# Weights of four expert units and the first pass's token operands made by VectorE in feed-forward blocks 2 and 3

## The chip, the cores and the metric

One core of a Trainium2 chip runs the whole program. The metric is the device time in microseconds. TensorE does the matrix products, VectorE, ScalarE and GpSimd the elementwise work, and SyncE (SP) issues every DMA, in one queue, in order. In rows of the profile TensorE is PE (its weight loads PEld), VectorE DVE, ScalarE ACT, GpSimd POOL, and SP's queue SPq.

## The reference, cut to what matters

Three layers follow one another: a chunked attention, a gated feed-forward layer, and a mixture of eight experts that is balanced over all tokens and so needs the logits of all of them.

```python
# attention: 4 batches, 8 heads, 768 positions, 64 wide; chunks of 32 with a window and 8 memory slots
x = softmax(q_c @ k_full.T / 8) @ v_full             # 3072 tokens x 512
# feed-forward, 512 -> 1536 -> 512
x = (sigmoid(x @ w_gate) * (x @ w_val)) @ w_out
# experts, 8 of them, 512 -> 1024 -> 512
P = exp(x @ w_gate2 - max)
for _ in range(8):                                    # balanced over rows and over all 3072 tokens
    P /= P.sum(1) + 1e-9;  P /= P.sum(0) + 1e-9;  P *= 3072 / 8
out = sum(P[:, e] * (relu(x @ w1[e]) @ w2[e]) for e in range(8))
```

## The kernel before, in words

**Precision.** Every float32 operand of a product is split in two: ScalarE writes the rounded high part, and VectorE or GpSimd subtracts it from the source for the low part (`operand`). A product is then three matmuls: high by high, high by low, low by high. Large products go by a scheme with seven products of half-sized blocks instead of eight, so sums and differences of blocks (`combine`) are made ahead of the splits. The seven operands have numbers 0 to 6.

**Stages.** Tokens come in eight chunks of 384. Attention of a chunk is four head pairs. The feed-forward layer works in blocks of two chunks: block 0 plainly, blocks 1, 2 and 3 by the seven products, each in six pairs of hidden columns. A pair b_p is a gate product, a value product (`strassen`), and one pair later the second product (`second`, banks px), whose drains VectorE adds into x2. Attention of the chunks ahead is spread over the blocks by `schedule`, which puts steps of a generator at counts of a clock that `hook` advances, some ten per pair. In block 1 the feed-forward weights are made and stored, in blocks 2 and 3 they are only loaded. A finished chunk of x2 is stored to DRAM (x2d), and its expert logits are made (pl, pm).

The experts come in three passes s of 1024 tokens. In a pass there are 32 units (expert, half, pair of columns); the first layer (`layer1`) makes seven products p of a unit, the second (`layer2` in pass 0, `layer2_turned` after it) takes two units at a time. In pass 0 each unit's raw weights are loaded (`ask`, tiles r), summed on VectorE (wq, wv), split by ScalarE and GpSimd, used, and stored in DRAM (w1k, seven tiles; w2k, four). Passes 1 and 2 load them from there (`w1_load`, w2_get). The token operands of a pass are made by `x_operands`: per pass four parts of 256 columns, each with four sums (xq) and seven splits (xl); the splits of operands 5, 1, 4 and 3 go to GpSimd, the others to VectorE. The balancing (`sinkhorn`) is a chain of small steps of VectorE with a matmul (pm, pb, pc) between them, one step every three products.

**Order.** A scheduler sets the order within each engine from its own timeline; the engines then run in that order and wait on semaphores. Attention's and the feed-forward layer's pools (c1) close at the end of block 3, and the experts' pools (c2) open in their memory, w2p, gg, ps_h and ps_y among them. The raw weights of pass 0 land in gg.

Of the kernel before, what the change touches and what calls it, by code (L numbers as in the profile page):

```python
# [10 lines left out]
F32 = mybir.dt.float32  # L11
# [48 lines left out]
def moe_chain(ctx: ExitStack, tc: tile.TileContext, qkv, mask, mrow, mone, wa, wg, wb, out):  # L60
# [66 lines left out]

    def w1_operands(nm, r, pool, kept=None, ce=None):
        a11, a12, a21, a22 = (r[i][:, kh * 256:(kh + 1) * 256] for i in range(2) for kh in range(2))
        t = w1_tiles(nm, pool)  # L130
        ge = nc.gpsimd
        ce = ce or ge
# [12 lines left out]
        return w1_sets(t)  # L145

    def w1_load(nm, pool, kept):
# [3 lines left out]
        return w1_sets(t)  # L151

    with ExitStack() as c1:
        wc = c1.enter_context(tc.tile_pool(name="wc", bufs=7))
        wp = c1.enter_context(tc.tile_pool(name="wp", bufs=6))
        un = c1.enter_context(tc.tile_pool(name="un", bufs=2))
        at = c1.enter_context(tc.tile_pool(name="at", bufs=2))
        cm = c1.enter_context(tc.tile_pool(name="cm", bufs=1))
        tq = c1.enter_context(tc.tile_pool(name="tq", bufs=5))
# [4 lines left out]

        wgs = cm.tile([128, KD, 2 * E], F32R, name="wgs")
        nc.scalar.copy(wgs[:, :, 0:E], wgate)
# [206 lines left out]
        def gated(nm, v, sg):  # L373
            nc.vector.tensor_tensor(out=v, in0=v, in1=sg, op=ALU.mult)
            gh = gp.tile([128, CT], F32R, tag="gh", name=f"gh{nm}")
            gl = gp.tile([128, CT], F32R, tag="gl", name=f"gl{nm}")
            operand(gh, gl, nc.vector, v)
            return gh, gl

        anchor = []  # L380
# [157 lines left out]
        def second(b, p, x2b, state, halves=(0, 1)):  # L538
            wo, gs = state
            for t in halves:  # L540
# [12 lines left out]
                if p == NPAIR - 1:  # L553
                    store_x2(2 * b + t, x2b[:, :, t, :])

        pend = []
# [58 lines left out]
    with ExitStack() as c2:  # L615
        sk = c2.enter_context(tc.tile_pool(name="sk", bufs=1))
        w2p = c2.enter_context(tc.tile_pool(name="w2p", bufs=8))
        gg = c2.enter_context(tc.tile_pool(name="gg", bufs=1))
        ps_h = c2.enter_context(tc.tile_pool(name="ps_h", bufs=4, space=PS))
        ps_y = c2.enter_context(tc.tile_pool(name="ps_y", bufs=4, space=PS))  # L620

# [51 lines left out]
        SW = 512  # L673
        SHB = 8

        def x_operands(s):
            xop = [[[slot("w" if i in (2, 3, 4) else "x", f"x{h}{s}_{i}_{kk}", 512, F32R) for kk in range(2)]
                    for h in "hl"] for i in range(7)]
            for kk in range(2):
                for o in range(0, 512, XW):  # L680
                    xr = rw.tile([128, 2, 2, XW], F32, tag="r", name=f"xs{s}_{kk}_{o}")
                    for kh in range(2):
                        for tb in range(2):
                            for q in range(0, XW, 128):
                                c, w = divmod(s * SB + tb * 512 + o + q, CT)
                                nc.sync.dma_start(out=xr[:, kh, tb, q:q + 128],
                                                  in_=x2d[c][:, 2 * kh + kk, w:w + 128])
                    b11, b12, b21, b22 = (xr[:, kh, tb, :] for kh in range(2) for tb in range(2))
                    xh = [xop[i][0][kk][:, o:o + XW] for i in range(7)]
                    xl = [xop[i][1][kk][:, o:o + XW] for i in range(7)]  # L690
                    ve = nc.vector
                    q = quad(f"xq{s}_{kk}_{o}")
                    combine(ve, q[:, 0], b12, b11, ALU.subtract)
                    combine(ve, q[:, 1], b22, q[:, 0], ALU.subtract)
                    combine(ve, q[:, 2], b22, b12, ALU.subtract)
                    combine(ve, q[:, 3], b21, q[:, 1], ALU.subtract)
                    for i, src in ((0, b11), (5, q[:, 1]), (1, b21), (6, q[:, 2]), (4, q[:, 0]), (2, b22), (3, q[:, 3])):
                        operand(xh[i], xl[i], nc.gpsimd if i in XP else ve, src)
            return xop
# [12 lines left out]
        def raw_pair(nm, src):  # L712
            rs = []
            for f, k in enumerate(("sh", "sl")):
                rs.append(gg.tile([128, 512], F32, tag=k, name=f"{nm}_{f}", bufs=SHB))
# [27 lines left out]
        def w2_get(s, e, hf, fp):  # L743
            nm = f"{s}_{e}_{hf}_{fp}"
            kept = w2k[e, hf, fp]
            dh, dl = w2_tile(nm, "a"), w2_tile(nm, "b")
            if s == 0:
                rs = raws.pop((e, hf, fp))[1]
# [6 lines left out]
            nc.sync.dma_start(out=dh.bitcast(F32), in_=kept[0])  # L755
            nc.sync.dma_start(out=dl.bitcast(F32), in_=kept[1])
            th, tl = w2_tile(nm, "c"), w2_tile(nm, "d")
            nc.sync.dma_start(out=th.bitcast(F32), in_=kept[2])
# [3 lines left out]
        def g_tile(kind, nm):  # L762
            return gg.tile([128, 512], F32R, tag=kind, name=nm, bufs=DB if kind[0] == "d" else SHB)

# [13 lines left out]
        def layer1(s, e, hf, xop, gs, w2):  # L778
# [6 lines left out]
            for fp in range(2):  # L785
                nm = f"{s}_{e}_{hf}_{fp}"
                if s == 0:
# [59 lines left out]
        def layer2(s, e, hf, gs, w2, acc):  # L847
# [23 lines left out]
            for t in range(NTT):  # L871
# [10 lines left out]
                accumulate(t, acc[t], py, True)  # L882
                if t % 4 == 1:
                    w2_sums()
# [141 lines left out]
```

## Time and profile before

| | |
|---|---|
| median of three runs | 2708.83 us (2707.37 to 2710.35) |
| profiled execution, span from first to last instruction | 2714.6 us |
| busy: PE, PEld, DVE, ACT, POOL | 97%, 83%, 76%, 42%, 30% |
| DMA | 587 MB, 216 GB/s over the span |

The profiled execution lists its span alone; what lies around it is not in the trace. The span is itself 5.8 us above the median of the timed runs. The stages follow from the names in the timeline: feed-forward blocks 2 and 3 lie at about 450 to 785 us, pass 0 of the experts starts at 785 us, pass 1 at about 1460, pass 2 at about 2072. A busy share says little by itself, since matmuls overlap: what TensorE lost in a stretch is told by the number of matmuls in it beside the number in an undisturbed stretch of the same kind.

### The profile page before, as it was taken

The page shows a single profiled execution, that of the slowest core. Times are in us where ns is not written, and L with a number is a line of the kernel's source. Part 1 is how long each engine was busy: PE and PEld are TensorE (multiplying, and loading weights), DVE is VectorE, ACT ScalarE, POOL GpSimd, SP SyncE. Part 2 cuts the span into 40 slices and gives each one's busy share as a digit, 9 for nine tenths or more (in the row PEclk, how much of TensorE's full clock was granted, in tenths as well). Part 3 has the DMA queues.
Part 4 walks back from the last instruction along what each step waited for, and adds up shares of the span by engine and source line. Part 5 has one row for each costly group of instructions (what it writes and reads, how often), then busy time and mean ns, then how long its engine had stood idle before and what let it go on. Part 6 is the DMA issues. An engine that isn't in the chain of part 4 may idle for free.

```text
span 2714.6 us, 37960 instructions
## 1 busy us (share of the span) xinstructions
PE 2646.4 (97%) x12917; PEld 2241.2 (83%) x12917; DVE 2072.3 (76%) x3403; ACT 1130.5 (42%) x2516; POOL 820.3 (30%) x594
## 2 busy tenths in 40 slices
PE   8999999999978999999999999999999999999998
PEld 6898888999967888888888888888887887888887
DVE  7888788675588666666667788888788778888887
ACT  6666866664344334334334333233233332333232
POOL 0002441000045355455453322233234332323232
PEclk9899999999989999999999999999999999999999
DMA  5445677566558476676677556655666565556654
GB/s 203 161 164 207 230 244 256 191 199 206 183 199 288 176 265 244 223 270 242 223 257 248 183 214 228 227 186 201 230 231 226 213 232 201 188 216 233 218 177 171
DMA packets 260526, 586.97 MB, mean 216 GB/s; under 512 B 28873, under 2 KB 45961, under 8 KB 260332
## 3 DMA queue, kind: packets, MB, share of 16 engines
q1 hardware_dynamic: 260332, 584.54, 61.0%
q8 instruction: 102, 1.67, 0.3%
q14 instruction: 92, 0.75, 0.1%
HBM read 408.17 MB, written 176.26 MB: 215 GB/s over the span
## 4 chain that ended last, share of the span: by engine, by line
PE 85%; DVE 8%; DMA 4%; ACT 1%; issue 1%; SPq 0%; POOL 0%; DVEq 0%; ACTq 0%; POOLq 0%
PE p L802 10%; PE p L803 10%; PE p L804 10%; PE py L74 4%; PE pz L901 4%; PE py L75 4%; PE py L76 4%; PE pz L902 4%; PE pz L903 4%; PE pzr L903 3%; PE pzr L901 3%; PE pzr L902 3%; DMA w2b<-w2k 2%; PE px L75 2%; PE px L76 2%; PE px L74 2%
## 5 line engine op out<-in xcount | busy, mean ns | idle before, releaser
L802 PE MATMUL p<-xh,w 128*128 128x512 f32 x1344 | 521.3, 392 | 10.0 <-ACT ce L824 4.9
L803 PE MATMUL p<-xl,w 128*128 128x512 f32 x1344 | 525.9, 391 | 0.8 <-DVE xl L111 0.8
L804 PE MATMUL p<-xh,w 128*128 128x512 f32 x1344 | 520.4, 391 | 0.0
L802 PEld LDWEIGHTS p<-xh,w 128*128 128x128 f32 x1344 | 253.8, 189 | 65.0 <-ACT ce L824 5.8
L803 PEld LDWEIGHTS p<-xl,w 128*128 128x128 f32 x1344 | 253.9, 189 | 54.1 <-DVE xl L111 1.2
L804 PEld LDWEIGHTS p<-xh,w 128*128 128x128 f32 x1344 | 253.8, 189 | 53.4 <-DMA w<-w1k 0.2
L111 POOL TENSOR_TENSOR gl<-ce,gh 128x512 fp32r<-128x512 f32 x64 | 93.2, 1456 | 460.1 <-ACT gh L110 460.1
L909 DVE TENSOR_TENSOR acc<-pz,acc 128x512 f32<-128x512 f32 x248 | 169.7, 686 | 70.9 <-PE pz L903 68.8
L111 POOL TENSOR_TENSOR sl<-cb,sh 128x512 fp32r<-128x512 f32 x64 | 87.1, 1361 | 387.1 <-ACT sh L110 288.3
L74 PE MATMUL py<-w2a,gh 128*128 128x512 f32 x512 | 201.4, 393 | 0.8 <-DVE acc L864 0.8
L75 PE MATMUL py<-w2b,gh 128*128 128x512 f32 x512 | 200.6, 392 | 0.0
L76 PE MATMUL py<-w2a,gl 128*128 128x512 f32 x512 | 197.5, 391 | 0.0
L909 DVE TENSOR_TENSOR acc<-pzr,acc 128x512 f32<-128x512 f32 x248 | 164.7, 686 | 35.8 <-PE pzr L903 34.9
L824 ACT COPY ce<-p 128x512 f32<-128x512 f32 x96 | 56.3, 587 | 224.4 <-PE p L804 215.2
L111 POOL TENSOR_TENSOR w2d<-wv,w2c 128x1024 fp32r<-128x1024 f32 x32 | 77.8, 2430 | 208.5 <-ACT w2c L110 206.6
L864 DVE SCALAR_TENSOR_TENSOR acc<-py,logit,acc 128x512 f32<-128x512 f32 x112 | 80.0, 742 | 71.3 <-PE py L76 71.2
L111 POOL TENSOR_TENSOR xl<-xq,xh 128x256 fp32r<-128x256 f32 x36 | 30.8, 868 | 334.1 <-ACT xh L110 329.0
L818 ACT COPY cb<-p 128x512 f32<-128x512 f32 x96 | 55.8, 581 | 162.4 <-PE p L804 162.4
L807 DVE TENSOR_TENSOR cd<-p,ce 128x512 f32<-128x512 f32 x96 | 66.1, 689 | 68.8 <-ACT ce L824 65.2
L74 PEld LDWEIGHTS py<-w2a,gh 128*128 128x128 f32 x512 | 97.0, 189 | 21.3 <-DVE acc L864 1.2
L76 PEld LDWEIGHTS py<-w2a,gl 128*128 128x128 f32 x512 | 97.0, 189 | 20.3
L75 PEld LDWEIGHTS py<-w2b,gh 128*128 128x128 f32 x512 | 97.0, 189 | 20.0
(289 smaller groups left out, 7025.2 us busy)
## 6 DMA issues: line engine op xcount, KB each, us to landing
w<-w1k SPq DMA_DIRECT2D x448, 256.0 KB
w1k<-w SPq DMA_DIRECT2D x224, 256.0 KB
r<-in_wb SPq DMA_DIRECT2D x128, 256.0 KB
w2a<-w2k SPq DMA_DIRECT2D x64, 512.0 KB
w2b<-w2k SPq DMA_DIRECT2D x64, 512.0 KB
w2c<-w2k SPq DMA_DIRECT2D x64, 512.0 KB
w2d<-w2k SPq DMA_DIRECT2D x64, 512.0 KB
w_g<-wak SPq DMA_DIRECT2D x84, 256.0 KB
```

The source lines that it names most:

```text
L74: nc.tensor.matmul(ps, wh, xh, start=first, stop=False)
L75: nc.tensor.matmul(ps, wh, xl, start=False, stop=False)
L76: nc.tensor.matmul(ps, wl, xh, start=False, stop=last)
L111: return eng.tensor_tensor(out=l, in0=src, in1=h.bitcast(F32), op=ALU.subtract)
L802: nc.tensor.matmul(ps, wh[:, ks], xh, start=kk == 0 and not more, stop=False, skip_group_check=True)
L803: nc.tensor.matmul(ps, wh[:, ks], xl, start=False, stop=False, skip_group_check=True)
L804: nc.tensor.matmul(ps, wl[:, ks], xh, start=False, stop=kk == 1, skip_group_check=True)
L864: nc.vector.scalar_tensor_tensor(out=dst, in0=src, scalar=pe, in1=dst, op0=ALU.mult, op1=ALU.add)
L901: nc.tensor.matmul(ps, wh[:, ds], gh, start=fp == 0 and not more, stop=False, skip_group_check=True)
L902: nc.tensor.matmul(ps, wh[:, ds], gl, start=False, stop=False, skip_group_check=True)
L903: nc.tensor.matmul(ps, wl[:, ds], gh, start=False, stop=fp == 1, skip_group_check=True)
L909: nc.vector.tensor_tensor(out=a[q], in0=ps, in1=a[q], op=ALU.add)
```

## The change

Four things are edited.

1. The weights of the first four units (`EN`) are no longer made in pass 0. A generator `early_weights` runs for each of them in feed-forward blocks 2 and 3, from 16 clock counts after block 2's start (`EA`), one step every two counts (`EB`), ten steps a unit. It loads the raw tiles in four loads of 512 KB (each half twice), makes the eight sums and all low parts on VectorE and the high parts on ScalarE, and stores all eleven tiles. In pass 0 these units' tiles are loaded; the other 28 units are made as before.
2. The token operands of pass 0 are made in two portions, all low parts on VectorE. Operands 0, 1 and 5 (`first_x`) are made in block 3 from count 40, and the other four (`rest_of_x`) at the end of block 3. Each portion loads the four parts anew and makes the first two sums anew.
3. In passes 1 and 2 too, the low parts of operands 5, 1, 4 and 3 move from GpSimd to VectorE (`XALL`).
4. Attention's pools lie on the other side of the memory stack and close when block 3 starts; operands 0, 1 and 5 take that memory. The experts' pools get `reuse_waits="tile"`. The tiles sh and sl move, twelve of sixteen, to slots that the token operands leave.

`paced` puts each VectorE instruction of the early steps behind the last low part (gl) that `gated` has issued at that point of the program.

```diff
+XA, XB = 40, 4
+EA, EB, EN = 16, 2, 4
+XALL = True
...
+    def x_part(s, xop, kk, o, which=range(7)):
+        xr = rw.tile([128, 2, 2, XW], F32, tag="r", name=f"xs{s}_{kk}_{o}_{which[0]}")
...
+        combine(ve, q[:, 0], b12, b11, ALU.subtract)
+        combine(ve, q[:, 1], b22, q[:, 0], ALU.subtract)
+        if 6 in which:
+            combine(ve, q[:, 2], b22, b12, ALU.subtract)
+            combine(ve, q[:, 3], b21, q[:, 1], ALU.subtract)
+        for i, src in ((0, b11), (5, q[:, 1]), (1, b21), (4, q[:, 0]), (6, q[:, 2]), (3, q[:, 3]), (2, b22)):
+            if i in which:
+                h, l = (xop[i][n][kk][:, o:o + XW] for n in range(2))
+                operand(h, l, nc.gpsimd if i in XP and s and not XALL else ve, src)
...
-            operand(gh, gl, nc.vector, v)
+            mark[0] = operand(gh, gl, nc.vector, v).ins
...
+        def paced(gen):
+            while True:
+                with tc.issue_after(mark[0]):
+                    if next(gen, gen) is gen:
+                        return
+                yield
...
+        def early_weights(u):
...
+            def split(q, src, n, kept):
+                h = rw.tile([128, 1024], F32R, tag="r", name=f"eh{q}_{nm}")[:, 0:n]
+                l = rw.tile([128, 1024], F32R, tag="st", name=f"el{q}_{nm}", bufs=SB_)[:, 0:n]
+                operand(h, l, nc.vector, src)
+                for a, b, o, m in kept:
+                    nc.sync.dma_start(out=a, in_=h[:, o:o + m].bitcast(F32))
+                    nc.sync.dma_start(out=b, in_=l[:, o:o + m].bitcast(F32))
...
+            ld, (a11, a12, a21, a22) = raw(0)
+            yield
+            q = quad(f"eq0_{nm}")
+            combine(ve, q[:, 0], a21, a22, ALU.add)
+            combine(ve, q[:, 1], q[:, 0], a11, ALU.subtract)
+            combine(ve, q[:, 2], a11, a21, ALU.subtract)
+            combine(ve, q[:, 3], a12, q[:, 1], ALU.subtract)
+            yield
+            split("s", flat(q), 1024, [(k1[2], k1[3], 0, 512), (k1[4], k1[5], 512, 512)])
...
         for b in range(1, NCH // 2):
+            if b == 2:
+                schedule(clock[0] + EA, [paced(early_weights(u)) for u in early_units], EB * 10, range(0, 10 * EB, EB))
...
+            else:
+                c3.close()
+                early["xe"] = ctx.enter_context(tc.tile_pool(name="xe", bufs=1, side="right", reuse_waits="tile"))
+                schedule(clock[0] + XA, [paced(first_x())], XB, range(0, 4 * XB, XB))
...
+                if b == NCH // 2 - 1 and p == NPAIR - 1:
+                    schedule(clock[0], [rest_of_x()], 1, range(4))
...
-        w2p = c2.enter_context(tc.tile_pool(name="w2p", bufs=8))
-        gg = c2.enter_context(tc.tile_pool(name="gg", bufs=1))
+        w2p = c2.enter_context(tc.tile_pool(name="w2p", bufs=8, reuse_waits="tile"))
+        gg = c2.enter_context(tc.tile_pool(name="gg", bufs=1, reuse_waits="tile"))
...
-        raws, asked = {}, iter(units)
+        raws, asked = {}, iter(units[EN:])
...
-                if s == 0:
+                if s == 0 and units.index((e, hf, fp)) >= EN - 2:
                     ask()
-                    r1 = raws[e, hf, fp][0]
-                    w = w1_operands(nm, r1, ws, w1k[e, hf, fp], nc.vector)
+                if (e, hf, fp) in raws:
+                    w = w1_operands(nm, raws[e, hf, fp][0], ws, w1k[e, hf, fp], nc.vector)
                 else:
                     w = w1_load(nm, ws, w1k[e, hf, fp])
...
-        ask()
-        ask()
-        xop = x_operands(0)
+        xop = early["x"]
```

Where it moves instructions, at three places. First VectorE in pair 2_2 of block 2, before (gl2_1_0_1 is the last low part of pair 2_1, x2_2 the drains of the second product):

```order
L111 TENSOR_TENSOR gl2_1_0_1_6378<-cvb2_1_6266,gh2_1_0_1_6377 128x384
L504 TENSOR_TENSOR cva2_2_6625<-p1_v2_2_6635,cva2_2_6625 128x384
L374 TENSOR_TENSOR cva2_2_6625<-cva2_2_6625,cga2_2_6417 128x384
L550 TENSOR_TENSOR x2_2_6006<-px2_1_1_0_6575,x2_2_6006 128x384
L550 TENSOR_TENSOR x2_2_6006<-px2_1_1_1_6583,x2_2_6006 128x384
L111 TENSOR_TENSOR gl2_2_0_0_6645<-cva2_2_6625,gh2_2_0_0_6644 128x384
```

The same place of VectorE in the changed kernel (er is a raw tile, eq a sum, ehs and els high and low parts of the sums):

```order
L115 TENSOR_TENSOR gl2_1_0_1_6378<-cvb2_1_6266,gh2_1_0_1_6377 128x384
L118 TENSOR_TENSOR eq0_0_0_0_6496<-er0_0_0_0_6438 128x256 x2
L118 TENSOR_TENSOR eq0_0_0_0_6496<-eq0_0_0_0_6496,er0_0_0_0_6438 128x256
L118 TENSOR_TENSOR eq0_0_0_0_6496<-er0_0_0_0_6438,eq0_0_0_0_6496 128x256
L554 TENSOR_TENSOR cva2_2_6642<-p1_v2_2_6652,cva2_2_6642 128x384
L415 TENSOR_TENSOR cva2_2_6642<-cva2_2_6642,cga2_2_6417 128x384
L600 TENSOR_TENSOR x2_2_6006<-px2_1_1_0_6590,x2_2_6006 128x384
L115 TENSOR_TENSOR els_0_0_0_6555<-eq0_0_0_0_6496,ehs_0_0_0_6554 128x1024
L600 TENSOR_TENSOR x2_2_6006<-px2_1_1_1_6598,x2_2_6006 128x384
L115 TENSOR_TENSOR gl2_2_0_0_6662<-cva2_2_6642,gh2_2_0_0_6661 128x384
```

A group of early instructions has come between a pair's last low part and the next pair's work; there are sixteen such groups in blocks 2 and 3.

Second TensorE where block 3 ends and pass 0 begins, before (pl6 and pl7 are the logits of the last two chunks, pm6 and pm7 their transposes, pm and pb the balancing's first two matmuls, p0 the first product of unit 0):

```order
L351 MATMUL pl7_9295<-x2h7_3_9328,wgs_587 16x384
L357 MATMUL pm6_9316<-ident_58,lg6_9314 128x16 x3
L351 MATMUL pl7_9295<-x2l7_3_9329,wgs_587 16x384
L357 MATMUL pm7_9336<-ident_58,lg7_9334 128x16 x3
L627 MATMUL pm_9592<-ident_58,m1_9564 1x128
L632 MATMUL pb_9626<-m2_9594,ones_63 128x1
L802 MATMUL p0_0_0_0_0_9562<-xh0_0_0_9383,w1_0_0_0_0_0_9531 128x512
L803 MATMUL p0_0_0_0_0_9562<-xl0_0_0_9385,w1_0_0_0_0_0_9531 128x512
```

And TensorE there in the changed kernel, from the logits' middle on:

```order
L392 MATMUL pl6_9658<-x2h6_2_9671,wgs_587 16x384
L392 MATMUL pl6_9658<-x2l6_2_9672,wgs_587 16x384
L392 MATMUL pl6_9658<-x2h6_3_9684,wgs_587 16x384
L922 MATMUL p0_0_0_0_0_9764<-xh0_0_0_9057,w1_0_0_0_0_0_9746 128x512
L923 MATMUL p0_0_0_0_0_9764<-xl0_0_0_9059,w1_0_0_0_0_0_9746 128x512
L924 MATMUL p0_0_0_0_0_9764<-xh0_0_0_9057,w1_0_0_0_0_1_9747 128x512
```

The first products of unit 0 have moved ahead of the last logits and of the balancing's first matmuls.

Third SP's queue at the same seam, before (x2d7 is the store of the last chunk, r1 and r2 the raw weights of pass 0):

```order
L343 DMA x2d7_77<-x2_3_8005 512x1x384
L716 DMA r1_0_0_0_0_9367<-in_wb 128x512
L716 DMA r1_0_0_0_1_9369<-in_wb 128x512
L716 DMA r2_0_0_0_0_9371<-in_wb 128x512
L716 DMA r2_0_0_0_1_9373<-in_wb 128x512
```

And in the changed kernel (w1 are tiles of the first layer, w2a and w2b of the second; the xs1 loads are for pass 1):

```order
L384 DMA x2d6_76<-x2_3_8131 512x1x384
L179 DMA xs1_0_0_0_15523<-x2d2_72 128x128
L871 DMA w2a_0_0_0_0_9851<-w2k0_0_0_0_416 128x1024
L872 DMA w2b_0_0_0_0_9852<-w2k0_0_0_1_417 128x1024
...
L872 DMA w2b_0_0_1_1_10345<-w2k0_1_1_1_429 128x1024
L384 DMA x2d7_77<-x2_3_8131 512x1x384
...
L154 DMA w1_0_0_0_1_2_9857<-w1k0_0_1_2_201 128x512
```

The raw loads behind the last store are gone; unit 0's first-layer tiles and two of unit 1's stand further up, among the loads of pair 3_5, and eight second-layer loads of 512 KB stand ahead of unit 1's other tiles.

## Rows read from the trace of the kernel before

**Rows 1.** The page's first part: span, busy time and share of each engine.

```profile
span 2714.6 us, 37960 instructions
PE 2646.4 (97%) x12917; PEld 2241.2 (83%) x12917; DVE 2072.3 (76%) x3403; ACT 1130.5 (42%) x2516; POOL 820.3 (30%) x594
```

**Rows 2.** Busy time by stretch: start and end, length, each engine's us (instructions); clock, DMA.

```profile
200.00:250.00 50.00, 50.00 (x319) 45.83 (x318) 45.04 (x93) 33.61 (x102) 6.00 (x5) 1.00 0.53 190
260.00:450.00 190.00, 180.15 (x1178) 162.07 (x1178) 157.52 (x297) 134.73 (x380) 70.04 (x53) 1.00 0.70 240
528.00:715.00 187.00, 185.28 (x1161) 176.12 (x1160) 115.66 (x231) 91.38 (x234) 0.00 (x0) 1.00 0.63 203
605.00:630.00 25.00, 23.28 (x144) 20.94 (x140) 20.84 (x44) 12.17 (x25) 0.00 (x0) 1.00 0.52 172
655.00:755.00 100.00, 100.00 (x579) 99.72 (x578) 55.20 (x104) 36.07 (x80) 6.30 (x8) 1.00 0.54 173
760.00:785.40 25.40, 15.93 (x63) 11.59 (x62) 18.09 (x39) 10.66 (x28) 6.14 (x7) 0.72 0.47 147
785.40:890.00 104.60, 90.61 (x363) 72.34 (x364) 87.04 (x159) 44.50 (x80) 57.66 (x40) 0.90 0.74 271
890.00:990.00 100.00, 100.00 (x443) 82.73 (x443) 64.35 (x101) 38.51 (x68) 44.39 (x30) 1.00 0.57 213
2050.00:2100.00 50.00, 45.76 (x185) 34.93 (x185) 41.57 (x66) 17.82 (x41) 22.71 (x22) 0.97 0.75 259
```

**Rows 3.** TensorE's waits from 755 to 890 us: total us, times, longest.

```profile
PE pc L646 <- DVE cs L643: 7.2, 3, 4.7
PE p L802 <- ACT ce L824: 4.2, 1, 4.2
```

**Rows 4.** Timeline of TensorE at the seam: start, us, then idle before and releaser.

```profile
763.02 0.98 PE L74 MATMUL px<-gh,hwo 128*128 128x384 f32 x4 [2.69 <-ACT gh L110]
...
785.43 0.79 PE L802 MATMUL p<-xh,w 128*128 128x512 f32 x1 [2.40 <-ACT w L110]
```

**Rows 5.** Timeline of SP's queue at the seam.

```profile
777.32 0.52 SPq L343 DMA_DIRECT2D x2d<-x  x1
781.97 6.63 SPq L716 DMA_DIRECT2D r<-in_wb  x12
```

**Rows 6.** Timeline of VectorE from the last pairs of block 3 into pass 0.

```profile
746.84 0.56 DVE L504 TENSOR_TENSOR cgb<-p_g,cgb 128x384 f32<-128x384 f32 x1 [0.48 <-PE p_g L501]
...
747.62 0.76 DVE L111 TENSOR_TENSOR xl<-xs,xh 128x256 fp32r<-128x256 f32 x2 [0.23 <-ACT xh L110]
...
777.20 1.95 DVE L111 TENSOR_TENSOR x2l<-x,x2h 128x384 fp32r<-128x384 f32 x4
...
786.24 0.77 DVE L114 TENSOR_TENSOR wq<-r 128x256 f32<-128x256 f32 x1 [3.02 <-DMA r<-in_wb]
...
791.22 1.52 DVE L114 TENSOR_TENSOR wq<-r,r 128x256 f32<-128x256 f32 x1
...
839.26 0.42 DVE L114 TENSOR_TENSOR wq<-r,r 128x256 f32<-128x256 f32 x1
```

**Rows 7.** Groups by line and shape: busy us, mean ns of one, idle before.

```profile
L111 DVE TENSOR_TENSOR lw<-w,hw 128x512 fp32r<-128x512 f32 x36 | 24.6, 683 | 2.5 <-ACT hw L110 2.5
L550 DVE TENSOR_TENSOR x<-px,x 128x384 f32<-128x384 f32 x120 | 63.1, 549 | 12.1 <-PE px L76 11.5
L114 DVE TENSOR_TENSOR wqg<-wl 128x256 f32<-128x256 f32 x12 | 4.5, 412 | 2.4 <-DMA wl<-wd 2.3
L111 POOL TENSOR_TENSOR xl<-xq,xh 128x256 fp32r<-128x256 f32 x36 | 30.8, 868 | 334.1 <-ACT xh L110 329.0
```

**Rows 8.** Busy time in three stretches of 10 us, columns as in rows 2.

```profile
660.00:670.00 10.00, 10.00 (x59) 10.00 (x58) 2.85 (x6) 3.21 (x8) 0.00 (x0) 1.00 0.92 302
790.00:800.00 10.00, 7.45 (x32) 5.32 (x30) 9.90 (x13) 4.66 (x10) 10.00 (x8) 1.00 1.03 394
920.00:930.00 10.00, 10.00 (x46) 8.28 (x45) 7.18 (x11) 4.43 (x8) 8.99 (x7) 1.00 1.03 400
```

More of the change, by code (lines that the diff above doesn't have):

```diff
@@ L151, in w1_load, with x_tiles, one @@
         return w1_sets(t)
+    early = {}
+    early_units = units[:EN]
+    def x_tiles(s, which):
+        def one(h, i, kk):
+            nm = f"x{h}{s}_{i}_{kk}"
+            if i in XE:
+                return early["xe"].tile([128, 512], F32R, tag=f"x{h}{i}{kk}", name=nm)
+            return slot("x", nm, 512, F32R)
+        t = {}
+        for i in (0, 5, 1, 4, 6, 3, 2):
+            if i in which:
+                t[i] = [[one(h, i, kk) for kk in range(2)] for h in "hl"]
+        return t
+    def x_part(s, xop, kk, o, which=range(7)):
+        xr = rw.tile([128, 2, 2, XW], F32, tag="r", name=f"xs{s}_{kk}_{o}_{which[0]}")
+        for kh in range(2):
+            for tb in range(2):
+                for q in range(0, XW, 128):
+                    c, w = divmod(s * SB + tb * 512 + o + q, CT)
+                    nc.sync.dma_start(out=xr[:, kh, tb, q:q + 128], in_=x2d[c][:, 2 * kh + kk, w:w + 128])
+        b11, b12, b21, b22 = (xr[:, kh, tb, :] for kh in range(2) for tb in range(2))
+        ve = nc.vector
+        q = quad(f"xq{s}_{kk}_{o}_{which[0]}")
+        combine(ve, q[:, 0], b12, b11, ALU.subtract)
[4 more added lines that the diff above has]
+        for i, src in ((0, b11), (5, q[:, 1]), (1, b21), (4, q[:, 0]), (6, q[:, 2]), (3, q[:, 3]), (2, b22)):
+            if i in which:
+                h, l = (xop[i][n][kk][:, o:o + XW] for n in range(2))
+                operand(h, l, nc.gpsimd if i in XP and s and not XALL else ve, src)
     with ExitStack() as c1:
@@ L554, in second, with raw @@
                     store_x2(2 * b + t, x2b[:, :, t, :])
+        parts = [(kk, o) for kk in range(2) for o in range(0, 512, XW)]
+        def early_weights(u):
+            nm = "_".join(map(str, u))
+            def raw(i):
+                ld = pair(f"er{i}_{nm}")
+                nc.sync.dma_start(out=ld, in_=wb[u[0], u[1], u[2], :, :, i, :])
+                return ld, [ld[:, r, o:o + 256] for r in range(2) for o in (0, 256)]
+            def split(q, src, n, kept):
[5 more added lines that the diff above has]
+                    nc.sync.dma_start(out=b, in_=l[:, o:o + m].bitcast(F32))
+            k1, k2 = w1k[u], w2k[u]
+            ve = nc.vector
+            ld, (a11, a12, a21, a22) = raw(0)
[7 more added lines that the diff above has]
+            split("s", flat(q), 1024, [(k1[2], k1[3], 0, 512), (k1[4], k1[5], 512, 512)])
+            yield
+            ld, q = raw(0)
+            yield
+            h = rw.tile([128, 1024], F32R, tag="st", name=f"ef_{nm}", bufs=SB_)
+            operand(h[:, 0:512], h[:, 512:], ve, ld[:, 0])
+            nc.sync.dma_start(out=k1[0], in_=h[:, 0:512].bitcast(F32))
+            nc.sync.dma_start(out=k1[1], in_=h[:, 512:].bitcast(F32))
+            h = rw.tile([128, 1024], F32R, tag="r", name=f"ea_{nm}")[:, 0:512]
+            operand(h[:, 0:256], h[:, 256:], ve, q[3])
+            nc.sync.dma_start(out=k1[6], in_=h.bitcast(F32))
+            yield
+            ld, (b11, b12, b21, b22) = raw(1)
+            yield
+            v = quad(f"eq1_{nm}")
+            combine(ve, v[:, 0], b12, b11, ALU.subtract)
+            combine(ve, v[:, 1], v[:, 0], b22, ALU.subtract)
+            combine(ve, v[:, 2], b22, b12, ALU.subtract)
+            combine(ve, v[:, 3], b21, v[:, 1], ALU.add)
+            yield
+            split("t", flat(v), 1024, [(k2[2], k2[3], 0, 1024)])
+            yield
+            ld, _ = raw(1)
+            yield
+            split("d", flat(ld), 1024, [(k2[0], k2[1], 0, 1024)])
+            yield
@@ L556, in moe_chain, with first_x, rest_of_x @@
+        def first_x():
+            early["x"] = x_tiles(0, XE)
+            for kk, o in parts:
+                x_part(0, early["x"], kk, o, XE)
+                yield
+        def rest_of_x():
+            rest = tuple(i for i in range(7) if i not in XE)
+            early["x"].update(x_tiles(0, rest))
+            for kk, o in parts:
+                x_part(0, early["x"], kk, o, rest)
+                yield
         pend = []
         for b in range(1, NCH // 2):
+            if b == 2:
+                schedule(clock[0] + EA, [paced(early_weights(u)) for u in early_units], EB * 10, range(0, 10 * EB, EB))
@@ L673, in moe_chain @@
         SW = 512
-        SHB = 8
         def x_operands(s):
-            xop = [[[slot("w" if i in (2, 3, 4) else "x", f"x{h}{s}_{i}_{kk}", 512, F32R) for kk in range(2)]
-                    for h in "hl"] for i in range(7)]
+            xop = x_tiles(s, range(7))
             for kk in range(2):
                 for o in range(0, 512, XW):
[L681 to L698, printed above, removed]
+                    x_part(s, xop, kk, o)
             return xop
@@ L762, in g_tile @@
         def g_tile(kind, nm):
-            return gg.tile([128, 512], F32R, tag=kind, name=nm, bufs=DB if kind[0] == "d" else SHB)
+            if kind[0] == "s":
+                return s_tile(kind, nm, F32R)
+            return gg.tile([128, 512], F32R, tag=kind, name=nm, bufs=DB)
         def emit_g(nm, src, kind, gate=None, pool=False):
@@ L882, in layer2 @@
                 accumulate(t, acc[t], py, True)
-                if t % 4 == 1:
+                if t % 4 == 1 and late:
                     w2_sums()
```

36 lines of the change are left out of this document (24 added, 12 removed).

## The prediction

> **What bounds the kernel now.** I read the page's first part first: TensorE is busy 97% of a span of 2714.6 us [rows 1]. That says little, so I looked for stretches with fewer matmuls than an undisturbed one. Two undisturbed stretches give the pitch: 100 us of block 3 hold 579 matmuls, 0.173 us each, and 100 us of pass 0 hold 443, 0.226 us each [rows 2]. Against these, three places lose time.
>
> The first and largest is the seam between block 3 and pass 0. From 760 to 785.4 us there are 63 matmuls, worth 63 x 0.173 = 10.9 us, so 14.5 of 25.4 us are lost. From 785.4 to 890 there are 363, worth 81.9 of 104.6 us, so 22.7 us are lost (some of the 363 are small ones of the balancing, so this is rather too little). Together 37 us, 1.4% of the span; the granted clock falls to 0.72 and 0.90 there, which is part of the same loss [rows 2].
>
> The timelines say why. The last chunk's store is issued at 777.32 and the first raw weights only at 781.97 [rows 5]; the first product p starts at 785.43, after a wait for ScalarE's half of a weight tile [rows 4]. VectorE, which has to sum the raw tiles, stands 3.02 us for the first of them, and while GpSimd makes its low parts a 128x256 sum takes 1.52 us, against 0.42 us of the same sum at 839 [rows 6]. GpSimd is busy 57.66 of these 104.6 us, VectorE 87.04 [rows 2]. The longest waits of TensorE there are on VectorE's chain of the balancing (pc, 7.2 us in three) and on ScalarE for a drain (4.2 us) [rows 3].
>
> The second place is the start of a later pass: from 2050 to 2100 us 185 matmuls stand where 221.5 would fit, 8.2 us lost. The third is small: 605 to 630 us in block 2, where VectorE is busy 20.84 of 25 us and TensorE misses 1.7 us [rows 2].
>
> **The change, part by part.** Durations are from one profiled execution, whose span is 5.8 us above the median of 2708.83; I take the difference in span and apply it to the median. VectorE's prices: 0.412 us for 128x256, 0.549 for 128x384, 0.683 for 128x512 [rows 7], so 0.136 us for each 128 columns, and by extension 1.23 us for 128x1024, a form that the trace does not have (an estimate). In a run of the same kind they follow closer: four of 384 in 1.95 us are 0.47 us each, two of 256 in 0.76 us are 0.35 each [rows 6].
>
> *Part a, the start of pass 0.* The raw loads, the sums and the splits of unit 0 go; its seven tiles are loaded among the loads of pair 3_5, and the first products stand ahead of the last logits. What now holds them is VectorE's order: from the last gate drain of block 3 (746.84 us [rows 6]) to the low part of x2 that precedes the first product I count 26 instructions of 384 columns and 35 of 256, the latter mostly rest_of_x. 26 x 0.47 + 35 x 0.35 = 24.4 us, and some 3 us for waits like the 2.69 us for gh at 763.02 [rows 4]: the first product at about 774, 11 us earlier than 785.43. Bounds: 14 if the waits vanish, 5 if the drains of x2, which wait for px, spread as before (the four low parts of the last chunk began at 777.20 [rows 6]).
>
> *Part b, from there to 890.* Units 0 to 3 need no VectorE and no GpSimd for weights, and the first of the other 28 is asked for two units ahead. Of the 22.7 us lost I let 8 remain: the balancing's chain with its 7.2 us of waits, which is still there and meets less to hide behind, and unit 1's tiles, since eight second-layer loads of 512 KB (4.2 MB, 11 us at the 394 GB/s seen at 790 [rows 8]) stand ahead of most of them in SP's queue. So -15; bounds -20 (only the balancing's 2 to 3 us left) and -8.
>
> *Part c, what blocks 2 and 3 pay.* On VectorE a unit costs 8 sums x 0.41, three low parts of 1024 columns x 1.23, and 0.68 + 0.41 for the two smaller ones: 8.1 us, 32 us for four. In 528 to 715 us, where the four units lie, VectorE has 115.66 of 187 us; with 32 more it has 148, 79%. From 200 to 250 us it has 45.04 of 50 (90%) and TensorE loses nothing [rows 2], so the load alone costs nothing, except at 605 to 630: 20.84 plus its share of 4.3 us is the whole 25 us, and I add 2 us. The 20 instructions of first_x, 8 us, fall in block 3, where VectorE has 55.20 of 100 us [rows 2]: nothing.
>
> The transfers are the larger question. A unit loads 2 MiB and stores 3.75 MiB, 6.03 MB; four are 24.1 MB in those 187 us, beside the 203 GB/s x 187 us = 38.0 MB of before: 62.1 MB, or 332 GB/s. The row has 203 GB/s at a busy share of 0.63, which scales to 322 GB/s at a full share: 193 us, 6 us late. Yet the 10 us stretches with large transfers have 394 and 400 GB/s at 1.03 [rows 8], 383 to 388 at a full share; at that price the new bytes take 63 us of transfer time beside 0.63 x 187 = 118, and 181 us are enough. So 0 to 6 us, if the queue never runs dry; I take 6, since stores of tiles just made come in bursts and weights of the blocks queue behind them. A stretch at 0.92 and 302 GB/s without loss [rows 8] says that a high share alone is harmless for 10 us. Part c is 6 + 2 = +8; bounds 0 (nothing shows) and +36 (only 87% of 322 GB/s reached, rival 1). The Trainium skill, "DMA: Bandwidth & Descriptors", Specifications, gives a limit of about 358 GB/s per core between memory and SBUF; by it the 62.1 MB would take 173 us, part c would be 2 and the time 2686 (an estimate). The rows of 394 and 400 GB/s stand above that figure, though for 10 us only.
>
> *Part d, passes 1 and 2.* Sixteen low parts a pass go from GpSimd (0.868 us each [rows 7], 13.9 us) to VectorE (16 x 0.35 = 5.6 us). They cost VectorE 5.6 us while it is 83% busy (41.57 of 50 [rows 2]), and they free it of GpSimd's disturbance: if five sums are spared the 1.1 us by which the disturbed one is longer [rows 6], 5.5 us come back. I take +1 for both passes; bounds -8 (TensorE's 8.2 us in part regained, twice 4) and +8.
>
> Sum: -11 - 15 + 8 + 1 = -17. 2709 - 17 = **2692 us**, a profiled span near 2698.
>
> **The rivals.** 0.2%, 5.4 us, is about what a measurement of this kernel can tell from no change.
>
> *Rival 1, slower: the transfers saturate in blocks 2 and 3.* If the mix reaches less than 296 GB/s, the 62.1 MB need over 210 us, 23 us late, and the whole gain of 26 less 3 is gone. At 280 GB/s (87% of 322) they need 222, 35 us late: -26 + 35 + 2 + 1 = +12, **2721**. For it: the demand, 332, lies above the scaled 322, and SP issues in order, so a weight load that is late holds the ones behind it. Against it: rows at 394 and 400 GB/s.
>
> *Rival 2, no change: VectorE stands for raw tiles.* Each unit has four loads, and sums in VectorE's order ahead of the next pair's drains; a load that lands late stops the drains too, and then p. In block 1, where weights are made from raw loads in just this way, TensorE loses 9.85 of 190 us at a share of 0.70 [rows 2]. At 10 to 20 us in addition, 14 say: **2706**. Against it: 200 to 250 us.
>
> *Rival 3, no change: the seam's loss moves.* rest_of_x stands on VectorE ahead of the last chunk's drains, and unit 1 waits behind 4.2 MB. With a at -5 and b at -8 the sum is -4: **2705**.
>
> *Rival 4, more:* the transfers fit, a is -14, b -20, c 0, d 0: **2675**.
>
> **How the numbers follow.** The forecast (2683 to 2703) gets 0.52, rival 4 0.13, rivals 2 and 3 together 0.17, rival 1 0.18. So faster 0.65, same 0.17, slower 0.18. The range runs from 2678, which leaves 0.07 of rival 4 below it, to 2716, where rival 1 at 286 GB/s stands (217 us, 30 late), with 0.12 above. The forecast's own range is 2683 to 2703.
>
> **What the profile after would show.** Right: the first p near 774 from the start of the span, less what blocks 2 and 3 lost (774 + 8 = 782 by the clock, with the last pair's px 8 us later than before too); some 12 of the 37 us lost at the seam left; GpSimd idle until unit 4's weights; 320 to 340 GB/s in blocks 2 and 3, with TensorE missing some 8 us there; the same loss as before at 2050. Wrong: a fall of TensorE's count in blocks 2 and 3 by more than 20 us' worth, with waits on weight loads (rival 1) or on VectorE behind a sum that waits for a raw tile (rival 2); or a first product that still comes 20 us after the last px (rival 3). The weakest step is the transfers' rate, then the 8 us that I leave in part b.

## The result, and the profile after

The changed kernel takes **2728.25 us** (median of four runs, 2726.62 to 2733.97) against 2709.32 of the kernel before: ratio 1.0074, interval [1.0059, 1.0089]. It is slower by 18.9 us, where 17 us less were forecast.

The page's first part of the changed kernel:

```profile
span 2726.8 us, 38049 instructions
PE 2655.2 (97%) x12917; PEld 2228.1 (82%) x12917; DVE 2060.8 (76%) x3479; ACT 1129.2 (41%) x2508; POOL 712.7 (26%) x518
```

Busy time by stretch, changed kernel (columns as in [rows 2]); the fourth row is as long as the stretch from 785.40 to 890 there, but begins with the first product, which now stands at 776.2:

```profile
528.00:715.00 187.00, 182.25 (x1136) 173.38 (x1135) 137.77 (x276) 101.51 (x246) 0.00 (x0) 1.00 0.88 313
605.00:630.00 25.00, 21.82 (x134) 19.62 (x133) 23.77 (x50) 12.99 (x26) 0.00 (x0) 1.00 0.60 195
655.00:755.00 100.00, 96.41 (x545) 95.57 (x544) 64.20 (x131) 37.48 (x77) 0.00 (x0) 0.98 0.86 292
...
776.20:880.80 104.60, 91.21 (x400) 72.80 (x399) 60.34 (x144) 33.54 (x60) 15.15 (x12) 0.97 0.55 192
890.00:990.00 100.00, 100.00 (x439) 81.98 (x438) 71.63 (x101) 43.58 (x76) 56.23 (x38) 1.00 0.71 256
2050.00:2100.00 50.00, 46.72 (x197) 35.86 (x195) 43.77 (x84) 18.52 (x42) 10.05 (x7) 1.00 0.71 239
```

The row to look at is the undisturbed one, 890 to 990. TensorE is busy for all of its 100 us in both kernels and waits for nothing, yet 439 matmuls lie in it and not 443. A busy share does not show this; the count does (400 us of pass 0, in the lines of the experiments below, hold 1766 before and 1750 after).

To see where the time went I set the two traces side by side by the number of matmuls that TensorE has begun. Both have 12,917. Changed kernel minus kernel before, at the start of the N-th matmul (the third column is the first experiment below):

| matmul | place | changed | with 192 bytes |
|---|---|---|---|
| 3000 | block 2, just ahead of the early units | -7.5 us | -9.7 |
| 4400 | late in block 3 | -4.0 | -4.6 |
| 5200 | pass 0, behind the seam | -13.0 | -13.0 |
| 7200 | pass 0, near its end | -8.8 | -13.0 |
| 7800 | pass 1 begun | -2.6 | -10.4 |
| 10000 | pass 1, near its end | +5.3 | -8.4 |
| 12800 | pass 2, near its end | +14.9 | -6.5 |
| last | | +12.2 | -8.4 |

The first -7.5 us are not the change's: nearly all of them arise in the first 110 us, and a later run of the very instructions of the kernel before (e5) gained 6 us there as well. What differs there is the granted clock: 0.91 over these 110 us in the kernel before, 0.94 in e5 and 0.95 in the changed kernel. In this order:

```profile
0.00:110.00 110.00, 96.53 (x542) 79.51 (x543) 85.94 (x181) 69.79 (x251) 0.70 (x6) 0.91 0.55 188
```
```profile
0.00:110.00 110.00, 98.08 (x578) 82.34 (x579) 91.54 (x193) 72.65 (x256) 0.70 (x6) 0.94 0.56 195
```
```profile
0.00:110.00 110.00, 98.29 (x586) 82.14 (x587) 92.79 (x195) 73.34 (x258) 0.70 (x6) 0.95 0.57 196
```

So the profiled execution of before was a long one by some 6 to 7 us, as its span beside the median had hinted, and from matmul 3000 on the changed kernel loses 12.2 + 7.5 = 19.7 us, near the 18.9 of the timed runs. From matmul 3000 to 4400, the rest of blocks 2 and 3, 3.5 us are lost; the seam gives 9.0 back; and from there on 25.2 us are lost, in all three passes, 6.2 of them in the 600 matmuls around the start of pass 1. For all of this the prediction's sum has +1 (part d, for passes 1 and 2).

A matmul here reads two tiles, one of 128x512, called its row below, and one of 128x128, its weights. TensorE's timeline in pass 0 of the changed kernel, two products of six matmuls without a gap:

```profile
1011.57 0.39 PE L922 MATMUL p<-xh,w 128*128 128x512 f32 x1
...
1012.97 0.39 PE L77 MATMUL py<-w2a,gh 128*128 128x512 f32 x1
...
1022.40 0.39 PE L922 MATMUL p<-xh,w 128*128 128x512 f32 x1
...
1023.76 0.39 PE L922 MATMUL p<-xh,w 128*128 128x512 f32 x1
```

The first six, of operand 0, take 1.40 us; the second six, of operand 3, take 1.36. I paired every matmul of the trace with the built program's list of where its tiles lie. Between 900 and 2680 us the 1582 matmuls counted whose 128x512 row is an operand 0, 1 or 5 begin 233.3 ns apart in the mean; all matmuls of the kernel before, 226.7 to 226.8. The program's list says what is peculiar to those tiles: they start 224 bytes behind a multiple of 256 (the memory that attention left, counted from the right end), and every other operand of these matmuls, rows and weights, 32 bytes behind one. After each run of slow matmuls the first of the others keeps its pace, and the four behind it are late, by 8.6, 1.9, 5.3 and 3.6 ns, 19.4 together. With 1728 matmuls at 6.6 ns and 361 such runs this makes 11.4 + 7.0 = 18.4 us.

### The profile page after: what moved, and what is told of

Read it like the earlier page. It is cut to its first block, busy times and chain, and to the rows that moved or that the text cites. A ratio compares the mean times of both kernels' runs of the same rounds, so it can differ in the third digit from the quotient of the medians.

```text
span 2726.8 us, 38049 instructions
## 1 busy us (share of the span) xinstructions
PE 2655.2 (97%) x12917; PEld 2228.1 (82%) x12917; DVE 2060.8 (76%) x3479; ACT 1129.2 (41%) x2508; POOL 712.7 (26%) x518
## 4 chain that ended last, share of the span: by engine, by line
PE 82%; DMA 8%; DVE 7%; ACT 2%; issue 1%; SPq 0%; POOL 0%; DVEq 0%; ACTq 0%; POOLq 0%
PE p L922 10%; PE p L923 10%; PE p L924 10%; PE pz L1021 4%; PE pz L1022 4%; PE py L77 4%; PE pz L1023 4%; PE py L78 4%; PE py L79 4%; DMA w2b<-w2k 4%; PE pzr L1023 3%; PE pzr L1021 3%; PE pzr L1022 3%; PE px L78 2%; PE px L79 2%; PE px L77 2%
## 5 line engine op out<-in xcount | busy, mean ns | idle before, releaser
L115 POOL TENSOR_TENSOR w2b<-r,w2a 128x512 fp32r<-128x512 f32 x56 | 80.9, 1464 | 416.8 <-PE py L78 405.9
L944 ACT COPY ce<-p 128x512 f32<-128x512 f32 x96 | 56.4, 587 | 237.8 <-PE p L924 227.8
L115 POOL TENSOR_TENSOR sl<-cd,sh 128x512 fp32r<-128x512 f32 x64 | 89.1, 1392 | 193.3 <-DVE sl L115 50.7
L115 POOL TENSOR_TENSOR w2d<-wv,w2c 128x1024 fp32r<-128x1024 f32 x28 | 67.4, 2406 | 237.0 <-ACT w2c L114 237.0
```

The costliest lines, as they stand in the source:

```text
L115: return eng.tensor_tensor(out=l, in0=src, in1=h.bitcast(F32), op=ALU.subtract)
```

## The experiments

**e1 to e4: is it the place of the tiles?** The theory (A) is that where a row starts sets TensorE's pace. The rivals are that end of the memory, and the low parts that moved to VectorE. In e1 to e3 one line reserves bytes above operands 0, 1 and 5; no instruction changes its place in any engine's order.

```diff
+                ctx.enter_context(tc.tile_pool(name="pad", bufs=1, side="right")).tile([128, 48], F32, name="pad")
                 early["xe"] = ctx.enter_context(tc.tile_pool(name="xe", bufs=1, side="right", reuse_waits="tile"))
```

e2 has `[128, 16]`, e3 `[128, 32]`. e4 is the kernel before with the 48 numbers reserved ahead of its pool `big`, so that everything moves.

> The changed kernel with 192 bytes reserved above operands 0, 1 and 5 of the token, so that their tiles start 192 bytes lower (32 bytes behind a multiple of 256, as every other operand, and not 224). Theory A (where such a row starts sets TensorE's pace): their matmuls go from 233.3 ns to the 226.7 ns of the others, 1728 of them and the slow ones behind each run of them, so some 17 us less: about 2711. Rival (the place at the top of the memory, or TensorE's company there): they stay at 233 ns and the time at 2728. Rival (the loss of 17 us in the three passes is the low parts that moved to VectorE): the same, 2728.

> The same with 64 bytes: the tiles start 160 bytes behind a multiple of 256, 32 behind a multiple of 128. Theory A: fast (226.7 ns, time near that with 192 bytes) if the step that counts is 128 bytes or if only the last bytes ahead of a multiple of 256 are slow; slow (233 ns, 2728) if only 32 behind a multiple of 256 is fast. Rival (place): 233 ns, 2728.

> The same with 128 bytes: the tiles start 96 bytes behind a multiple of 256 and of 128. Theory A: slow (233 ns, 2728) if the step is 128 bytes, fast (226.7 ns, about 2711) if only the last bytes ahead of a multiple of 256 or more are slow. Rival (place): 233 ns, 2728.

> The kernel before with 192 bytes reserved below its large pool, so that every tile from there on starts 192 bytes higher, 224 behind a multiple of 256, and nothing else changes. Theory A: the experts' 8255 matmuls of 512 columns slow to 233 ns, some 55 us, and those of 384 columns perhaps too, up to 30 us more: 2764 to 2794. Rivals: 2709, no pace changes.

Measured: e1 2709.93 us (11 runs) beside 2710.13, ratio 1.0008 [0.9996, 1.0019] (the ratio is taken over all runs, not from the two medians): the 18 us are gone. e2 2724.68 and e3 2726.45 (one run each): they stay. e4 2716.17, one run, and no matmul of 512 columns slower (its last matmul begins 0.2 us ahead of that of the kernel before, trace against trace): the forecast of 55 us more fell. So a start at 224 is not slow in itself; in e4 all operands start there. That made theory A2: what counts is the difference between the starts of the two operands of one matmul, within 256 bytes.

**e5, e9, e10: the difference, tested in the kernel before.** e5 and e10 reserve 192 and 32 bytes between the second layer's weights w2 and pool gg (gh, gl, sh, sl), e9 192 bytes below w2, so that w2 and gg move together.

```diff
+        c2.enter_context(tc.tile_pool(name="pad", bufs=1)).tile([128, 48], F32, name="pad")
         gg = c2.enter_context(tc.tile_pool(name="gg", bufs=1))
```

> The kernel before with 192 bytes reserved in the experts' stage between the second layer's weights and the gated operands (pool gg), so that gh, gl, sh and sl start 224 bytes behind a multiple of 256 and all else stays at 32; no instruction changes its place. Theory A2 (TensorE slows where the two operands of a matmul, the 128x512 row and the 128x128 weights, start at different places within 256 bytes): the second layer's matmuls py, pz and pzr go from 226.7 to 233 ns, 4224 of them, 28 us and some more behind each run, 2738 to 2750; the first layer's p stay at 226.7. Rival (only where the 128x512 row starts counts, against everything else in the memory): py, whose row is w2 and does not move, stay at 226.7, pz and pzr slow down, about 2728. Rival (only the right end of the memory is slow): nothing changes, 2709.

> The kernel before with the 192 bytes one pool lower than in the run with gg alone: w2 and gh, gl, sh, sl all start 224 bytes behind a multiple of 256, gh and the others at the very addresses that they had in that run; x and w1 stay at 32. Theory A2 (the two operands of one matmul against each other): every matmul has equal starts within 256 bytes again, py, pz, pzr and p all at 226.7 ns, time 2709. Rival (a row that starts at 224 is slow against the rest of the memory, or this part of the memory is slow): pz and pzr stay at 233 ns, about 2728.

> As the run with gg alone, with 32 bytes: gh, gl, sh, sl start at 64 of 256, w2 at 32. Theory A2 says that a difference of 32 bytes is a difference too: py, pz, pzr slower than 226.7, by some 2 to 7 ns as with 64, 128 and 192, 2718 to 2738. Rival (only differences of 64 bytes and more count): 226.7 and 2709.

Measured: e5 2734.03, e9 2721.58, e10 2740.72 us (one run each). No time fell in the range of its theory: e5 lies 4 us below it, e10 3 above, e9 13 above what it forecast; it is the pace of each kind of matmul that tells the theories apart. Start to start of the matmuls from 900 to 2680 us, those of 200 to 245 ns, by the start of the row less that of the weights within 256 bytes:

| kernel | matmuls | difference | mean ns |
|---|---|---|---|
| before, e4 | all | 0 | 226.7 to 226.8 |
| changed | p of operands 0, 1, 5 | 192 | 233.3 |
| e2 | the same | 128 | 231.8 |
| e3 | the same | 64 | 232.0 |
| e1 | the same, all others too | 0 | 226.7 to 226.9 |
| e5 | pz, pzr | 192 | 233.2 |
| e5 | py | 64 | 229.0 |
| e10 | pz, pzr | 32 | 233.2 to 233.3 |
| e10 | py | 224 | 233.0 |
| e9 | pz, pzr | 0, but at 224 where p is at 32 | 229.2 |
| e9 | py | 0, but at 224 where p is at 32 | 227.8 |
| e9 | p | 0 | 229.7 |
| changed, e2, e3, e5, e10 | all others | 0, mixed with the slow ones | 227.2 to 229.3 |

Every difference but 0 is slow, 32 bytes too. That 256 bytes are the period, e1 shows: there some p, pz, pzr and py have starts that differ by 256, 512 or 768 bytes within 1024, and all have 226.6 to 227.2 ns. py in e5 settles which operand counts: its row w2 did not move, only its weights gh, and it slowed. It is the matmul's own pair that counts, and not its row beside the weights that are loaded for the next one: in e5 the last p ahead of a py keeps 226.0 ns, and the last py ahead of a p has 229.0. e9 met neither expectation. With the addresses of e5's gh, but w2 beside them, pz falls from 233.2 to 229.2, so the rival of the slow place is out; yet 226.7 is not reached, and p is slow, which did not move at all. By its place in a run the loss stands in the first nine or ten matmuls after a change between p and the others (a p has 234.0 ns in the fourth place, 227.3 from the tenth on). So a change of the start from one matmul to the next costs as well, some 21 ns for each of the 900 changes between 900 and 2680 us. The counts of matmuls in an equal stretch of pass 0 (only p and py) and of pass 2 (p, pz and pzr) show the same in the profile; before, changed, e1, e5, e9, e10:

```profile
1000.00:1400.00 400.00, 400.00 (x1766) 331.33 (x1765) 260.41 (x398) 159.20 (x277) 202.01 (x135) 1.00 0.68 244
2200.00:2600.00 400.00, 396.50 (x1739) 325.39 (x1738) 330.64 (x484) 120.43 (x208) 121.28 (x85) 1.00 0.58 206
```
```profile
1000.00:1400.00 400.00, 400.00 (x1750) 327.98 (x1749) 261.33 (x390) 155.91 (x271) 196.78 (x136) 1.00 0.66 239
2200.00:2600.00 400.00, 396.58 (x1721) 321.55 (x1720) 315.55 (x473) 117.97 (x205) 111.95 (x83) 1.00 0.58 210
```
```profile
1000.00:1400.00 400.00, 399.51 (x1763) 330.60 (x1762) 261.33 (x393) 156.96 (x274) 199.14 (x137) 1.00 0.67 243
2200.00:2600.00 400.00, 395.36 (x1732) 323.88 (x1731) 316.39 (x475) 117.97 (x205) 112.11 (x83) 1.00 0.57 206
```
```profile
1000.00:1400.00 400.00, 400.00 (x1755) 329.30 (x1754) 254.03 (x389) 155.97 (x270) 201.57 (x136) 1.00 0.67 240
2200.00:2600.00 400.00, 396.62 (x1710) 319.56 (x1710) 322.41 (x473) 118.21 (x205) 120.13 (x83) 1.00 0.57 207
```
```profile
1000.00:1400.00 400.00, 400.00 (x1752) 328.52 (x1751) 253.81 (x388) 156.22 (x271) 202.67 (x136) 1.00 0.67 240
2200.00:2600.00 400.00, 395.66 (x1719) 321.62 (x1718) 325.03 (x477) 117.49 (x204) 119.42 (x82) 1.00 0.57 205
```
```profile
1000.00:1400.00 400.00, 400.00 (x1736) 325.51 (x1735) 255.38 (x389) 152.97 (x265) 197.69 (x133) 1.00 0.66 239
2200.00:2600.00 400.00, 397.71 (x1712) 320.30 (x1711) 320.56 (x470) 117.75 (x204) 116.83 (x81) 1.00 0.58 211
```

**e6 to e8: the parts of the change, with the 192 bytes of e1.** e6 undoes part 3, e7 part 1, and e8 makes the first portion of the token operands with the second:

```diff
-XALL = True
+XALL = False
```
```diff
-EA, EB, EN = 16, 2, 4
+EA, EB, EN = 16, 2, 0
...
+        ask()
+        ask()
         xop = early["x"]
```
```diff
-                schedule(clock[0] + XA, [paced(first_x())], XB, range(0, 4 * XB, XB))
...
-                    schedule(clock[0], [rest_of_x()], 1, range(4))
+                    schedule(clock[0], [first_x(), rest_of_x()], 1, range(4))
```

> The changed kernel with the 192 bytes, and the low parts of operands 5, 1, 4 and 3 of passes 1 and 2 on GpSimd again (part 3 undone). If that part costs what the trace after shows at the two starts of a pass beyond the slow matmuls, some 2 to 4 us in all: 2706 to 2708. Rival (the prediction's +1, or nothing): 2709 to 2710.

> The changed kernel with the 192 bytes and no unit's weights made early (EN 0, two raw units asked for ahead of pass 0 as before); token operands early. Theory (the early weights give the gain at the seam, and cost 5 us in blocks 2 and 3): the seam loses 8 us or more again, the blocks regain 5, about 2713. Rival (the token operands alone give it): about 2705.

> The changed kernel with the 192 bytes, the first portion of the token operands made at the end of block 3 with the second instead of from count 40 on; early weights kept. If the portion in block 3 is what lets pass 0 start at 772: VectorE has 20 low parts and sums more at the seam, 8 us later, about 2717. Rival (VectorE has room there): 2710.

Measured, beside 2708.09 of before: e6 2713.78, ratio 1.0023 [1.0010, 1.0036]; e7 2716.89, 1.0031 [1.0019, 1.0043]; e8 2703.88, 0.9988 [0.9975, 1.0001]. Against e1's 1.0008 the low parts on VectorE (e6) tend to save some 4 us, where I had charged 1 and expected of the run that undoing them would save; the two intervals overlap, so neither the size nor the sign is shown. The early weights (e7) save some 6 us, as their theory said. The early portion of the token operands (e8) costs some 5, though these intervals too overlap a little: both sides of my expectation fell. In e8's trace the 6 us are gained at the seam, between matmuls 4400 and 5200: 15.0 us against the kernel before. It is hardly the chance of one execution. The trace of e12 below, the same order of instructions, gains 14.0 there, and the five traces whose order is that of the changed kernel up to there (changed, e1, e2, e3, e6) gain 4.2 to 9.5. Nor is it the clock alone: from 750 to 850 us it is 0.98 in e8, and 0.98 in the changed kernel too.

**e11: the passage from block 2 to 3.** On e8, two early units in block 2 and two in block 3.

```diff
-                schedule(clock[0] + EA, [paced(early_weights(u)) for u in early_units], EB * 10, range(0, 10 * EB, EB))
+                schedule(clock[0] + EA, [paced(early_weights(u)) for u in early_units[:2]], EB * 10, range(0, 10 * EB, EB))
+            elif b == 3:
+                schedule(clock[0] + EA, [paced(early_weights(u)) for u in early_units[2:]], EB * 10, range(0, 10 * EB, EB))
```

> The version with the 192 bytes and both portions of the token operands at the end of block 3, and the four early units in two twos: two from 16 counts after block 2's start, two from 16 counts after block 3's start, so that none falls on the passage from block 2 to 3, where VectorE was full. If the 4 us that blocks 2 and 3 lost there are VectorE's: 2700. Rival (it is the transfers, or the clock): 2704 as without.

Measured: 2718.72 us, 1.0045 [1.0032, 1.0059], worse than either side. Between matmuls 3600 and 4000, around the passage, it loses 2.9 us against before, as e8 does, and the seam breaks: from 770 to 800 us e8 and then e11 have

```profile
770.00:785.00 15.00, 14.10 (x68) 9.77 (x66) 8.26 (x22) 5.41 (x13) 0.00 (x0) 1.00 0.99 357
785.00:800.00 15.00, 12.36 (x47) 9.65 (x48) 11.77 (x28) 8.41 (x14) 0.00 (x0) 0.89 0.83 260
```
```profile
770.00:785.00 15.00, 7.68 (x24) 3.71 (x23) 12.36 (x37) 8.09 (x20) 0.00 (x0) 0.60 0.48 135
785.00:800.00 15.00, 7.97 (x18) 5.67 (x19) 11.09 (x35) 4.23 (x10) 0.00 (x0) 0.50 0.81 257
```

115 matmuls against 42, at a granted clock of 0.60 and 0.50, the lower of the two levels (1.2 GHz) for most of the 30 us. TensorE's waits there are on the balancing (pc, 8.1 us in two) and on token operands (3.9 us in four). With the units in block 3, VectorE makes an early low part as late as 765.01 us, and so comes to the token operands later.

**e12: starts at multiples of 64, and e8's version once more.** e8 with 32 bytes reserved below pool `big` and 160 in place of 192 above operands 0, 1 and 5.

> The version with both portions of the token operands at the end of block 3, with 32 bytes reserved below the large pool and 160 instead of 192 above operands 0, 1 and 5: both operands of every matmul start 64 bytes behind a multiple of 256, and not 32. Theory A2 (only the difference between the two counts): pace 226.7 ns and the time of the same version without it, 2704, which also measures that version once more. Rival (a start at a multiple of 64 counts by itself): every large matmul shorter by up to 11 ns, as far as 512 columns at 2.4 GHz (213.3 ns) leave room, up to 90 us less.

Measured: 2705.75 us beside 2709.36, ratio 0.9986 [0.9974, 0.9998]; pace 226.7 to 226.9 ns. The common start itself does not count. It is the version of e8 measured a second time: 0.12 and 0.14% below the kernel before, the one interval reaching to 1.0001, the other staying below 1. Of all that ran it is the fastest. It is clearly faster than the changed kernel; its gain on the kernel before, 3 to 4 us, is less than the 5.4 us that the prediction takes as the least that can be told from no change.

## Why the prediction was wrong

**The step that failed: part 4 of the change has no term in the sum.** The prediction adds up what the moved work and the transfers cost, parts a to d, and puts the move of the pools at nothing, without a reason; where in the memory operands 0, 1 and 5 come to lie is not asked. That costs 18 us of the 18.9, shown by e1, which gives the same instructions with those tiles 192 bytes lower. Without it the change is worth about nothing (1.0008), and not the -17 of the sum; so the other terms were off as well. Rival 1 gave a slower kernel, 2721, but by the transfers: that the result is slower does not speak for it.

**Part b, the 22.7 us behind the first product, was mis-sized.** I let 8 remain. With the prediction's own reckoning, 104.6 us from the first product hold 400 matmuls, worth 90.3 us: 14.3 remain, so -8 and not -15. That is still too favourable, since small matmuls of the logits, which stood ahead of the first product, are now among the 400. By matmul numbers the whole seam gave 9.0 us (8.4 in e1) where a and b promised 26, so 28 of the 37 us are left and not 12. The waits of TensorE there are those of [rows 3] again:

```profile
PE pc L772 <- DVE cs L769: 8.5, 2, 6.0
PE p L922 <- ACT ce L944: 3.7, 2, 2.5
```

And the timeline of VectorE says what is late now:

```profile
813.30 0.43 DVE L118 TENSOR_TENSOR wq<-r 128x256 f32<-128x256 f32 x1 [4.98 <-DMA r<-in_wb]
...
818.00 0.49 DVE L769 TENSOR_REDUCE cs<-logit 128x8 f32<-128x192 f32 x1
...
860.29 0.43 DVE L118 TENSOR_TENSOR wq<-r 128x256 f32<-128x256 f32 x1 [2.03 <-DMA r<-in_wb]
```

The wait for the first raw tile, 3.02 us at 786 in [rows 6], has not gone with the early units. It stands 27 us later, at unit 4, and is longer, and steps of the balancing are behind it in VectorE's order (cs at 818.00, on which pc waits); TensorE's wait for pc is 8.5 us, where it was 7.2. Rival 3 named the right place and the loaded tiles of unit 1 as the cause; those cost 0.4 us (one wait for w).

**Part a came at its weak bound.** The first product stands 51.7 us behind matmul 4400 and not 56.8: 5 us earlier, in e1 8 (bounds 5 to 14). The forecast place, 782 by the clock of before, was met only because blocks 2 and 3 lost less: 776.25 + 7.5 = 783.8.

**Part c lay within its bounds, at half its size, and with the wrong half.** Blocks 2 and 3 lost 3.5 us, 5.1 in e1 (forecast 8); in the five traces with one order up to there it is 2.6 to 6.3. The transfers, for which I had 6 of the 8, reach 313 GB/s at a share of 0.88, 356 at a full share, between the two rates that I had, and no stretch of them loses matmuls for it: from 630 to 715, at 348 GB/s and a share of 0.97, 491 matmuls stand where 492 did. Rival 1 did not come. The limit of about 358 GB/s per core that the prediction cites from the Trainium skill ("DMA: Bandwidth & Descriptors", Specifications) lets the transfers fit as well, and this stretch agrees with it; the 394 and 400 GB/s of [rows 8] still stand above it. What is lost lies where VectorE was full, at 605 to 630 (134 matmuls for 144), and from 600 to 640 the granted clock is 0.91 in e1, 1.00 in the kernel before and in the changed kernel. But e11, with no early unit there, loses as much as e8 at this place; the cause is not settled.

**Part d, +1, is not confirmed.** By the two ratios e6 says -4 for what moved to VectorE, of which not even the sign is shown, as said above. And from matmul 7200 to the end e1, whose matmuls keep their pace, loses 4.6 us against before. The waits of TensorE for w2b and w2a after 1420 us, before and then e1:

```profile
PE pzr L903 <- DMA w2b<-w2k: 6.1, 9, 1.7
PE pzr L901 <- DMA w2a<-w2k: 2.0, 4, 1.4
```
```profile
PE pzr L1024 <- DMA w2b<-w2k: 8.9, 13, 2.2
PE pzr L1022 <- DMA w2a<-w2k: 3.8, 5, 1.5
```

8.1 us have become 12.7. In e6, e7, e8, e11 and e12 they are 11.9 to 14.2, with part 3 and without it, with early weights and without; in e4, the instructions of the kernel before, 9.8. So neither part 3 nor part 1 seems to be the cause; what remains is part 4, the moved sh and sl and the waits by tile, which was not tried alone. Whether these waits are the 4.6 us is not shown either: e4 loses 3.1 in the same stretch, and e6, with much the same waits as e1, 10.2.

In sum for e1, from its one trace: blocks +5, seam -8, passes +5, about nothing, as timed; the changed kernel has 18 us of slow matmuls on top.

## What to carry to other kernels

When a change moves tiles, look where they start: compare the start of each matmul's row with that of its weights within 256 bytes, before and after, and keep the two equal, at one and the same start for all matmuls that follow each other. In a stretch in which TensorE is busy throughout, count the matmuls; this kernel lost 0.7% with no wait in any view. And work that is made ahead for the first few of many units can move the first wait for raw data to the next unit, as here to unit 4, so the gain is to be reckoned from there (loads asked for further ahead were not tried).

## What the runs showed of the hardware that was not expected

- TensorE's pace at 128x512 float32, with weights of 128x128, depends on the starts of its two operands against each other: 226.7 to 226.9 ns where they are equal within 256 bytes in all matmuls of the kernel, 229.0 to 233.3 ns at differences of 32, 64, 128, 192 and 224 bytes. Both a moved row (e10's pz) and moved weights (e5's py) show it. Whether both start at 32, 64 or 224 does not matter (before, e12, e4).
- A change of the start from one matmul to the next costs as well: some 19 ns where a run of unequal starts ends in the changed kernel, in the second to the fifth matmul behind it, and some 21 ns where the common start changes in e9, spread over up to ten.
- Rows of 384 columns with weights of 128x128 were not tried at a difference. Why equality counts no run shows.
